# Order of the first weight loads, FFN1 by output column, and an event instruction for the last wait in a one-core decode kernel

## Chip, cores, metric

One core of one Trainium2 chip. The metric is the device time of one execution in microseconds (us), lower is better.

## The reference

A decode step: one new token for each of two sequences, with a key and value cache of 8192 positions, 32 heads of 128, and beside it a feed-forward block (FFN) on the same normed input.

```python
def reference(A_x, A_k_cache, A_v_cache, A_wq, A_wo, B_x, B_w1, B_w2):
    # x (2,1,512), caches (2,32,8192,128), wq (512,4096), wo (4096,512),
    # w1 (512,1792), w2 (1792,512), all bf16
    xn = _layernorm(A_x)
    # attention: q = xn@wq; softmax(q k^T / sqrt(128)) v; @wo
    # FFN: relu(xn@w1) @ w2
    return A_x + _A_ref(xn, A_k_cache, A_v_cache, A_wq, A_wo) + _B_ref(xn, B_w1, B_w2)
```

The caches are 268 MB of the 280.5 MB read. Each byte is used once.

## The kernel before

SyncE issues every large load, in order, on one queue. K and V come in tiles of 4 MB, one for a pair of heads, into two buffers each. TensorE transposes K, ScalarE and VectorE copy it back, TensorE makes scores and weighted values. wq borrows a V buffer, w1 and w2 share the buffer that wo takes at the end.

```python
    nc.sync.dma_start(w1_sb, B_w1.rearrange("(p kt) f -> p kt f", kt=KT)).then_inc(dW1, 16)
    nc.sync.dma_start(vs[1][:], A_wq.rearrange("(p kt) n -> p (kt n)", kt=KT)).then_inc(dV[1], 16)
    nc.scalar.dma_start(xsb[:], A_x.flatten_outer_dims()).then_inc(dX, 16)
    # SyncE, ...
        sp.dma_start(w2_sb, B_w2.rearrange("(p j) n -> p j n", j=FT)).then_inc(dW2, 16)
        load_k(0); load_k(1); load_v(0)
        for t in range(NP - 2):              # NP = 32 pairs of heads
            sp.wait_ge(pT[NG - 1], t + 1)    # K buffer transposed
            load_k(t + R)                    # R = 2
            sp.wait_ge(sW, t + 1)            # V buffer used
            load_v(t + 1)
        # ... last V in two halves, wo in five pieces, then the store of the output
    # GpSimd, at its end
        g.wait_ge(dO, 16)                    # the store has landed
        g.nop()
    # TensorE, before the loop over pairs (cut)
        pe.wait_ge(dW1, 16)
        w1_v = w1_sb.rearrange("p kt (f j) -> p kt j f", j=FT)     # step of 14 elements along f
        for g in range(FG):                                        # FFN1: w1 is the moving operand
            nj = min(4, FT - 4 * g)
            for kt in range(KT):
                i = pe.matmul(hp[:, 0:nj * P].rearrange("c (l f) -> c l f", f=P),
                    lhsT=xz[:, kt, Z - g * Bsz:Z - g * Bsz + FG * Bsz],
                    rhs=w1_v[:, kt, 4 * g:4 * g + nj, :], ...)
        pe.wait_ge(dV[1], 16)
        # ... 32 matmuls of q from wq; transposes of the hidden vector and of q; FFN2; then the loop
```

Of the kernel before, what the change touches and what calls it, by code (L numbers as in the profile page):

```python
# [7 lines left out]
ALU = mybir.AluOpType  # L8
# [11 lines left out]
def kernel(  # L20
# [12 lines left out]
    nc = tc.nc  # L33
    P = 128
    HP = P // 2
    bf16 = mybir.dt.bfloat16
    f32 = mybir.dt.float32

    Bsz, Sq, D = A_x.shape
# [3 lines left out]
    KT = D // P  # L43
    FT = Dff // P
# [7 lines left out]
    assert KT * H * Dh == SLOT  # L52
    QG = H * Dh // 512
    QH = 512 // Dh
    FG = (FT + 3) // 4
    Z = (QG - 1) * Bsz
    inv_sqrt = float(Dh) ** -0.5
    eps = 1e-5
# [3 lines left out]
    def sb(shape, dt, name):  # L62
        return ctx.enter_context(nc.sbuf_tensor(name, shape, dt))

    def ps(shape, dt, name):
        return ctx.enter_context(nc.psum_tensor(name, shape, dt))

    def sem(name):
        return tc.alloc_semaphore(name)
# [6 lines left out]
    w1_sb = w_sb[:, 0:KT * Dff].rearrange("p (kt f) -> p kt f", kt=KT)  # L76
# [3 lines left out]
    identb = sb([P, P], bf16, "identb")  # L80
# [12 lines left out]
    xz = sb([P, KT, 2 * Z + Bsz], bf16, "xz")  # L93
# [11 lines left out]
    OTn = sb([P, Bsz, H], bf16, "OTn")  # L105
    Ob = sb([H, Bsz, Dh], bf16, "Ob")
    OX = sb([P, WJ, Bsz], bf16, "OX")
    hb = sb([FG * Bsz, 512], bf16, "hb")
    hT = sb([P, 4, FG * Bsz], bf16, "hT")
    ys = sb([Bsz, D], f32, "ys")  # L110
    yT = sb([P, Bsz, KT], bf16, "yT")
    osb = sb([Bsz * KT, P], bf16, "osb")
# [1 line left out]
    tp = [ps([P, EG, P], bf16, f"tp{i}") for i in range(4)]  # L114
    Sc = [ps([P, 512], f32, f"Sc{i}") for i in range(2)]
    ot = [ps([P, 512], f32, f"ot{i}") for i in range(2)]
# [7 lines left out]
    def bc_of(i):  # L124
# [3 lines left out]
    dX, dO, dW1, dW2 = sem("dX"), sem("dO"), sem("dW1"), sem("dW2")  # L128
# [4 lines left out]
    sG, sI, sQ, sQ1 = sem("sG"), sem("sI"), sem("sQ"), sem("sQ1")  # L133
# [5 lines left out]
    sH, sF, sZ = sem("sH"), sem("sF"), sem("sZ")  # L139
# [11 lines left out]
    tpx = tp[0][:].rearrange("p g k -> p (g k)")[:, 0:KT * Bsz].rearrange(  # L151
        "p (kt b) -> p kt b", b=Bsz
    )
    hp = ot[1][0:FG * Bsz, :]
    tph = tp[2][:].rearrange("p g k -> p (g k)")[:, 0:4 * FG * Bsz].rearrange(
        "p (l c) -> p l c", l=4
    )
    y = Sc[1][0:Bsz, :]
    fin = ot[0][:, 0:KT * Bsz].rearrange("p (b c) -> p c b", c=KT)

# [4 lines left out]
    def load_v(t):  # L165
        nc.sync.dma_start(vs[t % R][:], V_all[t * P:(t + 1) * P, :]).then_inc(dV[t % R], 16)

    nc.sync.dma_start(w1_sb, B_w1.rearrange("(p kt) f -> p kt f", kt=KT)).then_inc(dW1, 16)
    nc.sync.dma_start(vs[1][:], A_wq.rearrange("(p kt) n -> p (kt n)", kt=KT)).then_inc(dV[1], 16)
    nc.scalar.dma_start(xsb[:], A_x.flatten_outer_dims()).then_inc(dX, 16)  # L170


    @(lambda f: f(nc.sync))
    def _(sp):
        sp.dma_start(w2_sb, B_w2.rearrange("(p j) n -> p j n", j=FT)).then_inc(dW2, 16)
        load_k(0)
        load_k(1)
        load_v(0)
        for t in range(NP - 2):
            sp.wait_ge(pT[NG - 1], t + 1)  # L180
            load_k(t + R)
            sp.wait_ge(sW, t + 1)
            load_v(t + 1)
        sp.wait_ge(sW, NP - 1)
        for i in range(2):
            sl = slice(i * SLOT // 2, (i + 1) * SLOT // 2)
            sp.dma_start(  # L187
                vs[(NP - 1) % R][:, sl], V_all[(NP - 1) * P:NP * P, sl]
            ).then_inc(dH[i], 16)
        for c in range(NC):  # L190
            sl = slice(cuts[c], cuts[c + 1])
            sp.dma_start(wo_sb[:, sl, :], wo_v[:, sl, :]).then_inc(dW[c], 16)  # L192
        sp.wait_ge(sE, 1)
        sp.dma_start(
            out.rearrange("b s (c p) -> (b s c) p", p=P), osb[:]
        ).then_inc(dO, 16)


    @(lambda f: f(nc.gpsimd))
    def _(g):  # L200
        g.memset(identb[:], 0.0).then_inc(sG, 1)
        g.memset(sel[:], 0.0).then_inc(sG, 1)
        g.memset(onesh[:], 0.0).then_inc(sG, 1)
        g.wait_ge(sG, 1)
        g.affine_select(
            out=identb[:], in_=identb[:], compare_op=ALU.not_equal, fill=1.0,
            base=0, pattern=[[-1, P]], channel_multiplier=1,
        ).then_inc(sI, 1)
        g.wait_ge(sG, 2)
        g.affine_select(  # L210
            out=sel[:], in_=sel[:], compare_op=ALU.not_equal, fill=1.0,
            base=0, pattern=[[-1, DQ], [1, P]], channel_multiplier=-DQ,
        ).then_inc(sI, 1)
        g.wait_ge(sI, 2)
        g.memset(prm[0][:], 0.0).then_inc(sG, 1)
        g.wait_ge(sG, 4)
        for u in range(2):
            g.memset(onesh[u * HP:(u + 1) * HP, u, :], 1.0).then_inc(sI, 1)
            g.wait_ge(sI, 3 + u)
        g.memset(ident2[:], 0.0).then_inc(sG, 1)  # L220
        g.wait_ge(sG, 5)
        g.affine_select(
            out=ident2[:], in_=ident2[:], compare_op=ALU.not_equal, fill=1.0,
            base=0, pattern=[[-1, Bsz]], channel_multiplier=1,
        ).then_inc(sI, 1)
        g.wait_ge(sV, 100)
        for t in range(NP):
            if t >= R:
                g.wait_ge(sS, t - R + 1)
            g.tensor_copy(q2[t % R][:], qb[:, 2 * t:2 * t + 2]).then_inc(sQ1, 1)  # L230
        g.wait_ge(dO, 16)
        g.nop()


    @(lambda f: f(nc.tensor))
    def _(pe):
        pe.wait_ge(sI, 1)
        pe.wait_ge(sV, 5)
        for kt in range(KT):
            i = pe.transpose(tpx[:, kt, :], xn[:, kt, :], identb[0:Bsz, 0:Bsz])  # L240
        i.then_inc(sQ, 1)
        pe.wait_ge(sV, 6)
        pe.wait_ge(dW1, 16)

        w1_v = w1_sb.rearrange("p kt (f j) -> p kt j f", j=FT)
        for g in range(FG):
            nj = min(4, FT - 4 * g)
            for kt in range(KT):
                i = pe.matmul(  # L249
                    hp[:, 0:nj * P].rearrange("c (l f) -> c l f", f=P),  # L250
                    lhsT=xz[:, kt, Z - g * Bsz:Z - g * Bsz + FG * Bsz],
                    rhs=w1_v[:, kt, 4 * g:4 * g + nj, :],
                    start=(g == 0 and kt == 0),
                    stop=(g == FG - 1 and kt == KT - 1),
                )
        i.then_inc(sF, 1)
        pe.wait_ge(dV[1], 16)
        for g in range(QG):
            for kt in range(KT):
                i = pe.matmul(  # L260
                    qp,
                    lhsT=xz[:, kt, Z - g * Bsz:Z - g * Bsz + QG * Bsz],
                    rhs=vs[1][:, (kt * QG + g) * 512:(kt * QG + g + 1) * 512],
                    start=(g == 0 and kt == 0),
                    stop=(g == QG - 1 and kt == KT - 1),
                )
        i.then_inc(sQ, 1)
        pe.wait_ge(sF, 2)
        for l in range(4):
            i = pe.transpose(  # L270
                tph[:, l, :], hb[:, l * P:(l + 1) * P], identb[0:FG * Bsz, 0:FG * Bsz]
            )
        i.then_inc(sF, 1)
        pe.wait_ge(sV, 7)
        for l in range(QH):
            i = pe.transpose(
                tpq[:, l, :], qs[:, l * Dh:(l + 1) * Dh], identb[0:QG * Bsz, 0:QG * Bsz]
            )
        i.then_inc(sQ, 1)
        pe.wait_ge(sF, 4)  # L280
        pe.wait_ge(dW2, 16)
        for j in range(FT):
            i = pe.matmul(  # L283
                y,
                lhsT=hT[:, j % 4, (j // 4) * Bsz:(j // 4 + 1) * Bsz],
                rhs=w2_sb[:, j, :],
                start=(j == 0),
                stop=(j == FT - 1),
            )
# [77 lines left out]
        pe.wait_ge(sP, NP + 1)  # L367
        pe.wait_ge(sO, NP + 1)
        pe.wait_ge(sI, 5)
        pe.wait_ge(sF, 6)  # L370
        dbp = Sc[0][:, 0:N].rearrange("p (t u) -> p t u", u=2)
        for u in range(2):
            t = pe.matmul(dbp[:, :, u], lhsT=onesh[:, u, :], rhs=RS[:], start=True, stop=True)
# [1 line left out]
        for k in range(KT):  # L375
            pe.matmul(
                fin[:, k, :],
                lhsT=ys[:, k * P:(k + 1) * P],
                rhs=ident2[:],
                start=(k == 0),  # L380
                stop=False,
# [13 lines left out]
        for dq in range(DQ):  # L395
            t = pe.matmul(
                ox,
                lhsT=sel[:, dq, :],
                rhs=Ob[:, :, dq * WJ:(dq + 1) * WJ],
                start=(dq == 0),  # L400
                stop=(dq == DQ - 1),
# [4 lines left out]
        for c in range(NC):  # L406
            pe.wait_ge(dW[c], 16)
            for j in range(cuts[c], cuts[c + 1]):
                for k in range(KT):
                    t = pe.matmul(  # L410
                        fin[:, k, :],
                        lhsT=wo_sb[:, j, k * P:(k + 1) * P],
                        rhs=OX[:, j, :],
                        start=False,
                        stop=(j == WJ - 1 and k == KT - 1),
# [13 lines left out]
    def _(v):  # L429
# [13 lines left out]
            out=xn[:],  # L443
            in0=xsb[:].rearrange("b (p kt) -> b kt p", kt=KT),
            scalar1=mv[:, 0:1],
            scalar2=rinv[:, 0:1],
            op0=ALU.subtract,
# [2 lines left out]
        v.wait_ge(sQ, 1)  # L450
        v.wait_ge(sZ, 1)
        v.tensor_copy(xz[:, :, Z:Z + Bsz], tpx).then_inc(sV, 1)
        v.wait_ge(sF, 1)
        v.tensor_scalar(  # L454
            out=hb[:], in0=hp, scalar1=0.0, scalar2=None, op0=ALU.max,
        ).then_inc(sF, 1)
        v.wait_ge(sQ, 2)

        v.tensor_scalar(  # L459
            out=qs[:], in0=qp, scalar1=inv_sqrt, scalar2=None, op0=ALU.mult  # L460
        ).then_inc(sV, 1)
        v.wait_ge(sF, 3)
        v.tensor_copy(hT[:], tph).then_inc(sF, 1)
        v.wait_ge(sQ, 3)

        v.tensor_copy(
            qb[:].rearrange("p (b g l) -> p l g b", b=Bsz, l=QH),
            tpq.rearrange("p l (g b) -> p l g b", b=Bsz),
        ).then_inc(sV, 93)
        v.wait_ge(sF, 5)  # L470
        v.tensor_tensor(out=ys[:], in0=y, in1=xsb[:], op=ALU.add).then_inc(sF, 1)

        def pair(i, n):
# [19 lines left out]
        with v.Fori(0, NP // R):  # L493
# [10 lines left out]
            out=on[:, 0:N - 2], in0=OTf[:, 2:N], in1=RD[:, 0:N - 2], op=ALU.mult  # L504
# [3 lines left out]
            out=on[:, N - 2:N], in0=ot[1][:, 0:2], in1=RD[:, N - 2:N], op=ALU.mult  # L508
# [81 lines left out]
```

## Time and profile before

| | before |
|---|---|
| median time, 3 runs | 661.67 us (661.57 to 661.88) |
| span of the profiled run | 659.7 us |
| last piece of wo landed | 655.86 us |
| from there to the end of the span | 3.86 us |

Times within a trace count from the span's start. In the page's slices one digit or number stands for a fortieth of the span. A line of the timeline gives start, length, engine, source line, operation and count; in brackets is the idle time before it and what ended it. The lines themselves stand in the prediction.

### The profile page before, as it was taken

What the parts mean: (1) busy time and instruction counts of PE and PEld (TensorE: products, weight loads), DVE (VectorE), ACT (ScalarE), POOL (GpSimd) and SP (SyncE); (2) the same over time, 40 slices, a digit from 0 to 9 for tenths busy, and PEclk for the clock granted to TensorE, in tenths of its full rate; (3) what the DMA queues carried; (4) which work ended last, traced back from release to release, by engine and by line L of the source; (5) the groups of instructions that cost most, each with busy time, mean ns of one, the idle gap of its engine ahead of it and who ended that gap; (6) DMA issues with size and microseconds to landing.
All of it is one profiled execution on the core that took longest, in us unless ns stands there. A gap on an engine that the chain in (4) does not pass through costs nothing.

```text
span 659.7 us, 26788 instructions
## 1 busy us (share of the span) xinstructions
PE 568.2 (86%) x12701; PEld 535.8 (81%) x12701; DVE 253.6 (38%) x437; ACT 255.8 (39%) x403; POOL 8.8 (1%) x46
## 2 busy tenths in 40 slices
PE   4998899979799788789878879978788898878897
PEld 0388898978798788789878879978788888878896
DVE  1154354424344333334433434443334443434341
ACT  1044445434434434244353433534243434433340
POOL 1000000000000000000000000000000000000000
PEclk9998999979999889898988998989899988989996
DMA  8999999999999999999999999999999999999996
GB/s 360 431 437 432 424 435 425 441 429 429 435 427 439 425 435 431 431 433 425 441 425 433 437 425 439 425 435 431 431 433 425 441 427 431 437 425 439 425 424 259
DMA packets 10542, 280.66 MB, mean 425 GB/s; under 512 B 1186, under 2 KB 1188, under 8 KB 1700
## 3 DMA queue, kind: packets, MB, share of 16 engines
q1 hardware_dynamic: 10528, 280.50, 99.0%
q8 instruction: 9, 0.15, 0.1%
q14 instruction: 1, 0.01, 0.0%
q10 hardware_dynamic: 4, 0.00, 0.0%
HBM read 280.50 MB, written 0.00 MB: 425 GB/s over the span
## 4 chain that ended last, share of the span: by engine, by line
DMA 59%; PE 37%; ACT 2%; issue 1%; SPq 0%; DVE 0%; ACTq 0%
DMA ks<-in_A_k_cache_dram 53%; PE tp L298 20%; PE Sc L305 10%; DMA w_sb<-in_A_wo_dram 4%; PE ot L318 3%; PE ot L249 2%; ACT kT L425 2%; PE ot L260 1%; DMA w_sb<-in_B_w_dram 1%; PE Sc L283 0%; ACT L425 0%; SPq L192 0%; SPq L187 0%; PE Sc L353 0%; DVE qs L459 0%
## 5 line engine op out<-in xcount | busy, mean ns | idle before, releaser
L298 PE MATMUL tp<-identb,ks 128*128 128x128 bf16 x4096 | 324.5, 229 | 70.1 <-DMA ks<-in_A_k_cache_dram 67.5
L425 DVE COPY kT<-tp 128x1024 bf16<-128x1024 bf16 x320 | 219.5, 691 | 322.4 <-PE tp L298 322.0
L298 PEld LDWEIGHTS tp<-identb,ks 128*128 128x128 bf16 x4096 | 255.7, 103 | 73.9 <-DMA ks<-in_A_k_cache_dram 70.7
L425 ACT COPY kT<-tp 128x1024 bf16<-128x1024 bf16 x192 | 194.3, 1012 | 236.2 <-PE tp L298 236.1
L305 PE MATMUL Sc<-q,kT 128*128 128x64 bf16 x4096 | 217.3, 196 | 6.5 <-ACT kT L425 5.6
L305 PEld LDWEIGHTS Sc<-q,kT 128*128 128x128 bf16 x4096 | 179.1, 100 | 10.0 <-ACT kT L425 9.1
L318 PE MATMUL ot<-prm,vs 128*128 128x64 bf16 x4224 | 157.4, 193 | 0.4 <-issue 0.4
L318 PEld LDWEIGHTS ot<-prm,vs 128*128 128x128 bf16 x4224 | 140.4, 98 | 3.2 <-issue 0.5
L540 ACT COPY nm<-Sc 128x2 f32<-128x2 f32 x32 | 5.1, 160 | 118.9 <-PE Sc L356 118.9
L544 ACT ACTIVATE prm<-Sc,nm 64x128 bf16<-64x128 f32 x64 | 25.7, 401 | 4.3
L481 DVE TENSOR_REDUCE mcol<-Sc 64x1 bf16<-64x128 f32 x64 | 18.6, 291 | 18.5 <-PE Sc L305 18.0
L425 ACT ACT_TABLE_LOAD x16 | 20.5, 1283 | 2.2
L486 DVE TENSOR_REDUCE mx<-Sc 1x2 bf16<-1x128 bf16 x32 | 8.9, 279 | 17.5 <-PE Sc L353 17.5
L249 PE MATMUL ot<-w_sb,xz 128*8 128x512 bf16 (+1 forms) x16 | 12.9, 975 | 3.0 <-DMA w_sb<-in_B_w_dram 3.0
L532 ACT COPY OTf<-ot 128x2 f32 x32 | 5.1, 160 | 22.4 <-PE ot L318 22.4
L230 POOL COPY q<-qb 128x2 bf16<-128x2 bf16 x32 | 5.8, 184 | 591.0 <-PE Sc L305 563.7
L249 PEld LDWEIGHTS ot<-w_sb,xz 128*8 128x8 bf16 x16 | 1.6, 104 | 13.4 <-issue 13.4
L544 ACT ACTIVATION_READ_ACCUMULATOR prm<-Sc,nm x64 | 11.8, 185 | 0.0
L260 PE MATMUL ot<-vs,xz 128*16 128x512 bf16 x32 | 8.2, 422 | 0.0
L260 PEld LDWEIGHTS ot<-vs,xz 128*16 128x16 bf16 x32 | 3.1, 98 | 5.4 <-issue 2.4
L353 PE MATMUL Sc<-identb,mcol 128*1 128x128 bf16 x32 | 7.0, 217 | 0.0
L454 DVE TENSOR_SCALAR hb<-ot 8x512 bf16<-8x512 f32 x1 | 0.7, 678 | 15.8 <-PE ot L249 15.8
(59 smaller groups left out, 39.5 us busy)
## 6 DMA issues: line engine op xcount, KB each, us to landing
ks<-in_A_k_cache_dram SPq DMA_DIRECT2D x32, 4096.0 KB, 26.7
vs<-in_A_v_cache_dram SPq DMA_DIRECT2D x31, 4096.0 KB, 31.3
vs<-in_A_wq_dram SPq DMA_DIRECT2D x1, 4096.0 KB, 17.0
vs<-in_A_v_cache_dram SPq DMA_DIRECT2D x2, 2048.0 KB, 19.0
w_sb<-in_B_w_dram SPq DMA_DIRECT2D x2, 1792.0 KB, 14.3
w_sb<-in_A_wo_dram SPq DMA_DIRECT2D x1, 1792.0 KB, 25.1
w_sb<-in_A_wo_dram SPq DMA_DIRECT2D x1, 896.0 KB, 26.8
w_sb<-in_A_wo_dram SPq DMA_DIRECT2D x1, 768.0 KB, 28.2
```

Source lines behind the costliest of these rows:

```text
L230: g.tensor_copy(q2[t % R][:], qb[:, 2 * t:2 * t + 2]).then_inc(sQ1, 1)
L249: i = pe.matmul(hp[:, 0:nj * P].rearrange("c (l f) -> c l f", f=P), lhsT=xz[:, kt, Z - g * Bsz:Z - g * Bsz + FG * Bsz], rhs=w1_v[:, kt, 4 ...
L260: i = pe.matmul(qp, lhsT=xz[:, kt, Z - g * Bsz:Z - g * Bsz + QG * Bsz], rhs=vs[1][:, (kt * QG + g) * 512:(kt * QG + g + 1) * 512], start=( ...
L298: t = pe.transpose(tp[e % 4][:, i, :], ks[r][:, kk * Dh:(kk + 1) * Dh], identb[:])
L305: t = pe.matmul(Sc[r][:, 2 * kk:2 * kk + 2 * REP], lhsT=kT[e % 4][:, i, :], rhs=rep(q2[r][:]), start=True, stop=True,)
L318: t = pe.matmul(ot[r][:, 0:2 * REP], lhsT=vs[r][:, kk * Dh:(kk + 1) * Dh], rhs=rep(prm[r][:, kk, :]), start=(kk == 0), stop=(kk == KB - 1),)
L353: pe.transpose(tr_of(r), mcol[r][:], identb[:]).then_inc(sT, 1)
L425: fn(kT[e % 4][:], tp[e % 4][:]).then_inc(kR[e], 1)
L481: m = v.tensor_reduce(out=mcol[i][half, :], in_=S_of(i)[half, :, u], axis=AX.X, op=ALU.max)
L486: v.tensor_reduce(out=mx[i][:], in_=tr_of(i).rearrange("o (u m) -> o u m", u=2), axis=AX.X, op=ALU.max, negate=True,).then_inc(sX, 1)
L532: a.copy(OTf[:, bass.ds(c, 2)], ot[r][:, 0:2]).then_inc(sO, 1)
L544: x = a.activation(out=prm[i][half, :, u], in_=S_of(i)[half, :, u], func=ACTF.Exp, bias=nm[i][half, u:u + 1], scale=1.0, accum_out=RS[half ...
```

## The change

The intent: q, which the attention needs, comes first; the FFN1 weights become the stationary operand, so that the hidden vector comes out already transposed (by column) and needs no transposes of its own; and the wait for the store is no longer carried by a branch.

```diff
-    nc.sync.dma_start(w1_sb, B_w1.rearrange("(p kt) f -> p kt f", kt=KT)).then_inc(dW1, 16)
     nc.sync.dma_start(vs[1][:], A_wq.rearrange("(p kt) n -> p (kt n)", kt=KT)).then_inc(dV[1], 16)
...
     def _(sp):
+        sp.dma_start(w1_sb, B_w1.rearrange("(p kt) f -> p kt f", kt=KT)).then_inc(dW1, 16)
         sp.dma_start(w2_sb, B_w2.rearrange("(p j) n -> p j n", j=FT)).then_inc(dW2, 16)
...
-        g.wait_ge(dO, 16)
-        g.nop()
+        g.wait_ge(dO, 16).then_inc(sG, 1)
...  (the FFN1 loop moves behind the q projection and becomes)
+        for j in range(FT):
+            for kt in range(KT):
+                i = pe.matmul(
+                    hp[:, j, :],
+                    lhsT=w1_v[:, kt, j, :],
+                    rhs=xz[:, kt, Z:Z + Bsz],
+                    start=(kt == 0),
+                    stop=(kt == KT - 1),
+                )
...  (its four transposes go; VectorE writes relu(hp) straight to hT, after q's eviction)
```

## The prediction

> **What bounds the kernel now.** I read the page first: its span, the busy shares, the slices and the queues.

> ```profile
> span 659.7 us, 26788 instructions
> ...
> PE 568.2 (86%) x12701; PEld 535.8 (81%) x12701; DVE 253.6 (38%) x437; ACT 255.8 (39%) x403; POOL 8.8 (1%) x46
> ...
> DMA  8999999999999999999999999999999999999996
> GB/s 360 431 437 432 424 435 425 441 429 429 435 427 439 425 435 431 431 433 425 441 425 433 437 425 439 425 435 431 431 433 425 441 427 431 437 425 439 425 424 259
> ...
> q1 hardware_dynamic: 10528, 280.50, 99.0%
> ```

> The reader is to see that every slice but the first and the last moves 424 to 441 GB/s and that one queue alone keeps the 16 engines busy for 99.0% of the span. TensorE is busy too (86%), so the next question is which of the two waits for the other. The view of waits answers it, first for the engines, then for the queue that issues the loads.

> ```profile
> PE tp L298 <- DMA ks<-in_A_k_cache_dram: 67.5, 27, 3.4
> ...
> SPq L163 <- PE tp L298: 435.8, 30, 40.7
> SPq L166 <- PE ot L318: 144.5, 30, 5.6
> ```

> TensorE waits 27 times for a K tile. The issuing queue waits for TensorE as well (a K buffer is reused once it has been transposed), but that is the issue, not the transfer: issued loads lie in the queue. What counts is whether the queue ever runs dry. The tightest places are early, and the timeline of the first 90 us shows them:

> ```profile
> 8.84 12.92 PE L249 MATMUL ot<-w_sb,xz 128*8 128x512 bf16 x16 [3.03 <-DMA w_sb<-in_B_w_dram]
> ...
> 21.58 8.23 PE L260 MATMUL ot<-vs,xz 128*16 128x512 bf16 x32
> ...
> 30.77 3.18 PE L283 MATMUL Sc<-w_sb,hT 128*2 128x512 bf16 x14
> ...
> 33.88 1.51 PE L298 MATMUL tp<-identb,ks 128*128 128x128 bf16 x24
> ...
> 44.82 0.33 SPq L163 DMA_DIRECT2D ks<-in_A_k_cache_dram  x1
> ...
> 53.91 0.73 PE L298 MATMUL tp<-identb,ks 128*128 128x128 bf16 x10 [2.61 <-issue]
> ...
> 65.25 0.33 SPq L163 DMA_DIRECT2D ks<-in_A_k_cache_dram  x1
> ```

> Six loads are issued at the start: w1, wq, w2, K0, K1, V0, together 2 x 1.835 + 4 x 4.194 = 20.45 MB. Data begins to flow at about 2.4 us (the windows show 8 GB/s before 2 us and 244 from 2 to 4). At 432 GB/s they last until 2.4 + 47.3 = 49.7 us. The next load, K2, is issued at 44.82, so 4.9 us of work was still in the queue. With K2 and V1 the queue has 28.84 MB and lasts until 69.2; K3 comes at 65.25, 3.9 us ahead. That is the smallest margin that I find; K4 comes at 83.17 and K5 at 99.02, with 37.2 and 45.6 MB issued, so some 5 and 9 us ahead. TensorE catches up until 99 us and waits for K in nearly every step from there. So the transfers set the time from 2.4 us until the last piece of wo lands. The chain of waits, read near the end, gives the rest:

> ```profile
> 627.04 28.82 DMA w_sb<-in_A_wo_dram
> 655.86 0.05 issue
> 655.91 0.39 PE ot L410 x8
> 656.29 0.02 issue
> 656.32 0.18 DVE yT L517
> 656.49 0.04 issue
> 656.54 0.28 PE tp L419
> ```

> The last load lands at 655.86, then a short serial tail runs to 659.72. The span is 1.95 us below the timed 661.67.

> [...] the slices average about 431. [...] the kernel has about 653.5 us between first and last byte, with instruction fetches and the uneven end of the 16 engines in it. [...] The trace before has no strided weight load; its packed ones with a moving width of 2 (L410) went at 84 in 2.36 us, 28 ns each. [...] The old FFN1 reads w1 as the moving operand with a step of 14 elements, 28 bytes[...]: 0.91 us for 512 columns, 1.78 ns a column, against 0.43 us for packed columns of the q projection just after it.

> **The change part by part.**
> First, the order of loads. The same bytes in the same number of loads; no byte leaves the queue, and the first issue stays at 0.96 us. Worth 0 on the transfer path. For TensorE it moves the first wait: w1 (1.835 MB) landed at 0.96 + 7.74 = 8.70; wq, first now, is 2.36 MB more, at 431 GB/s 5.5 us, so 14.2 us. w1 then lands where wq did, 1.43 + 17.0 = 18.4 us, and w2 stays.
> Second, TensorE's front part. From 14.2 us the 32 matmuls of q take about 8.7 us (8.23 in before with some six at 0.43 us and the rest at 0.215[...]), which ends at 22.9, after w1. Then FFN1: 56 loads of 128 weights with a step of 28 bytes, each with a matmul of 2 columns, in place of 16 wide matmuls (12.92 us), and no transposes of the hidden vector (0.25 us, and its 0.68 us eviction of 8x512 turns into one of 128x28, some 0.16 us as the small copies here). Two cases. [...] If not, 128 x 1.78 = 228 ns, 12.8 us. [...] After FFN1 come the q transposes, the eviction and FFN2: 0.25 + 0.4 + 3.2 = some 3.9 us, as the 4.1 us from 29.8 to 33.9 in before. K0's transposes begin at 22.9 + 3.2 + 3.9 = 30.0 us in the first case, 3.9 us earlier than 33.88; at 39.6 in the second, 5.7 later.
> On the path to the end, being 3.9 us earlier is worth nothing: K2 would be issued at about 41 us behind 8.8 us of queued work instead of 4.9. What TensorE gains it hands back as a longer wait for K, at the latest where it now catches up at 99 us.
> Third, the last wait. In the sequencers' records the 2 KB store's landing is complete at 658.28; GpSimd's compare-and-branch, which carries the wait, runs 658.305 to 658.338, and its next instruction, the NOP that releases the final barrier, stands at 658.467. That is 0.16 us from the branch's start. SyncE, whose last branches carry no wait, goes from the end of its store's issue (657.456) to its next instruction (657.501) in 0.045 us. With the wait on an event instruction (0.017 us in these records) and free branches behind it I reckon 0.06 us, so 0.1 us gained at the serial end, nothing beside it.
> Sum: 0 + 0 - 0.1. Prediction: 661.57, rounded to 661.6 us.

> **The rivals.**
> A: TensorE's front part is on the path. The chain of waits gives L249 2% and L260 1% of the span; whoever takes this as time to be had expects 4 to 10 us less, 652 to 658. Against it stand the flat GB/s row and the queue's backlog at 44.82; the chain only says what TensorE did while the transfers ran beside it.
> B: The strided weights go at the slow rate (or slower), and TensorE starts K0 5.7 us late. Then K2 is issued at 50.5 against 49.7, K3 at 71 against 69.2 (if the 2.61 us stall stays), and the queue runs dry for 1 to 2 us and some start-up: 663 to 665. For it: the w1 reads did cost 1.78 ns a column. Against it: [...] that q's start could hide part. I give it one in seven.
> C: The instruction fetches move. TensorE's program is some 72 instructions longer in front of the loop (40 more load-matmul pairs less 4 transposes), so the 2.61 us stall in the first pass and the 16 KB fetches among the data fall elsewhere. The early stall is hidden; a fetch on the last engine to finish could move the last landing by 0.6 us (16 KB at a sixteenth of 431 GB/s) either way: 661.0 to 662.2.
> D: The event instruction costs as much as the branch: 661.7.

> **Range and chances.** The three runs of before span 0.31 us. Around 661.6 I put C's and D's few tenths on both sides and a part of B above: 661.0 to 662.4. Over 2% faster means below 648.7[...]: excluded but for a misreading, 0.005. Over 2% slower means above 674.9, 13 us of dry queue, more than B makes: 0.01.

> **What would show it right or wrong.** The slices' GB/s stay at 424 to 441 and the last wo piece lands within 0.4 us of 655.86. The q matmuls start near 14.2 us. FFN1's 56 matmuls take near 3 us (first case) or near 13 us (second). K0's transposes start near 30 us; K2 is issued near 41, and TensorE's total wait for K grows by some 3 us. The gap from the store's landing to GpSimd's NOP shrinks from 0.19 to about 0.1 us. I am wrong if a slice early on falls below 420, if the last landing moves by more than 1 us, or if the tail after 655.86 changes by more than 0.3 us.

The 3.2 us for FFN1 in the first case stands as my estimate, which nothing in the trace before showed; with it the sum for K0 comes to 22.9 + 3.2 + 3.9 = 30.0 us. (The second case, "if not", takes the 1.78 ns that the trace has for a column at that step for each of 128 weights.) And the reason why 2% faster was excluded; an estimate from the trace does as well, since 280.5 MB at its 431 GB/s take 650.8 us, more than 648.7.

## The result

| | before | after |
|---|---|---|
| median of 6 runs | 661.62 us (661.37 to 661.88) | 660.84 us (660.68 to 661.06) |
| span of the profiled run | 659.72 | 658.64 |
| last piece of wo landed | 655.86 | 654.85 |
| from there to the end | 3.86 | 3.79 |

The ratio is 0.9989 (95% interval 0.9976 to 1.0002). A ratio is the mean time of one kernel's runs over that of the other's of the same rounds, so not quite the ratio of the medians quoted. 660.84 lies below my range. A second set of five runs of the same kernel (below) gave 660.84 again, ratio 0.9985 (0.9971 to 0.9998). Of the 1.08 us between the two spans, 1.01 is the earlier last landing and 0.07 the shorter tail.

The page after, the same parts as in the prediction:

```profile
span 658.6 us, 26859 instructions
...
DMA  8999999999999999999999999999999999999996
GB/s 365 430 444 418 439 430 429 432 428 442 422 442 424 436 428 432 432 428 444 420 442 428 432 430 430 434 430 442 424 436 428 432 432 428 440 424 442 426 424 281
...
q1 hardware_dynamic: 10528, 280.50, 99.2%
```

The stream of loads is as full as before. (A slice at 418 was to prove me wrong by my own text; these numbers swing by 20 and more from slice to slice, and counted by whole packets the 16 engines had work from 3.5 to 652 us in both traces.) The timeline of the front part after:

```profile
13.23 9.54 PE L240 MATMUL ot<-vs,xz 128*16 128x512 bf16 x32 [8.60 <-DMA vs<-in_A_wq_dram]
...
22.70 3.52 PE L253 MATMUL ot<-xz,w_sb 128*128 128x2 bf16 x56
...
26.50 5.84 PE L270 MATMUL Sc<-w_sb,hT 128*2 128x512 bf16 x14
...
32.77 1.51 PE L285 MATMUL tp<-identb,ks 128*128 128x128 bf16 x24 [0.43 <-DMA ks<-in_A_k_cache_dram]
...
43.72 0.33 SPq L158 DMA_DIRECT2D ks<-in_A_k_cache_dram  x1
```

FFN1 shrank from 12.92 to 3.52 us, 63 ns for each pair of weight load and matmul. But K0 begins only 1.1 us earlier: TensorE now waits for K0 itself, whose last part landed at 32.73. That none of this reaches the end, as forecast, is tested below. The chain of waits near the end says where the time came from:

```profile
625.73 29.12 DMA w_sb<-in_A_wo_dram
654.85 0.05 issue
654.90 0.39 PE ot L397 x8
```

The transfers end 1.01 us earlier, with the same bytes in the same number of loads (280.50 MB on the load queue in both) at the same rate (425 and 426 GB/s on average). The windows of the last four microseconds of transfer show it as well. Columns: window and its length, busy time (and count) of PE, PEld, DVE, ACT and POOL, granted clock, DMA share, GB/s. First before, then after:

```profile
652.00:653.00 1.00, 1.00 (x44) 1.00 (x41) 0.00 (x0) 0.00 (x0) 0.00 (x0) 0.50 0.88 336
653.00:654.00 1.00, 0.82 (x31) 0.73 (x28) 0.00 (x0) 0.00 (x0) 0.00 (x0) 0.50 0.50 195
654.00:655.00 1.00, 0.68 (x24) 0.68 (x24) 0.00 (x0) 0.00 (x0) 0.00 (x0) 0.50 0.26 92
655.00:656.00 1.00, 0.70 (x20) 0.53 (x18) 0.00 (x0) 0.00 (x0) 0.00 (x0) 0.50 0.05 20
```

```profile
652.00:653.00 1.00, 0.49 (x18) 0.40 (x14) 0.00 (x0) 0.00 (x0) 0.00 (x0) 1.00 0.83 326
653.00:654.00 1.00, 0.75 (x25) 0.67 (x25) 0.00 (x0) 0.00 (x0) 0.00 (x0) 0.57 0.51 201
654.00:655.00 1.00, 0.72 (x22) 0.56 (x18) 0.00 (x0) 0.00 (x0) 0.00 (x0) 0.50 0.21 70
655.00:656.00 1.00, 0.54 (x9) 0.27 (x8) 0.33 (x2) 0.00 (x0) 0.00 (x0) 0.50 0.00 0
```

In both the engines leave one by one from 652 us on. Before, a few drag on past 655; after, none does. It is not the stream that got faster but its slowest engine.

That can be read engine by engine: in the trace each large load has 16 landing records, as many as the profile counts DMA engines, and I read them as one for each. (Where a single landing is still out, in pool_fetch below, the DMA share is 0.06, one engine of 16.) Here they are (us, sorted; computed from the trace's landing events) for the first load and for the last piece of wo:

```
before, first load (w1):  7.23 7.29 7.30 7.33 7.38 7.40 7.49 7.58 7.65 7.70 7.81 7.88 8.24 8.62 8.64 8.70
after,  first load (wq): 12.70 12.79 12.86 12.89 12.90 12.91 12.93 12.94 12.95 12.96 12.97 12.98 12.99 13.00 13.07 13.09
before, last of wo: 652.98 652.99 653.08 653.09 653.36 653.37 653.42 654.31 654.45 654.50 654.62 654.77 655.05 655.44 655.84 655.86
after,  last of wo: 653.04 653.06 653.18 653.19 653.20 653.23 653.40 653.44 654.67 654.70 654.71 654.74 654.78 654.83 654.84 654.85
```

The first engine to finish wo does so at 652.98 and 653.04, no gain at all; the last at 655.86 and 654.85. The spread of the first load's landings is 1.47 us before and 0.39 after, a difference of 1.08; that of the last is 2.88 and 1.81, a difference of 1.07. In between the spread of before is 1.45 or 1.46 in the loads that land at 18 (wq), 23 (w2) and 32 us (K0). So an engine that starts late stays late: the 1.47 us at 8.70 us is still 1.45 or 1.46 at 32. (The landing records do not name the engine. That it is the same one is read from the distances between the 16 landings, which stay the same from load to load.)

The second feature of these rows is the step of about 1.3 us that splits the 16 landings of after into two groups. The trace has packets of 16 KB on an instruction queue. (I take them for TensorE fetching its program, from where they lie: in before one runs from 51.4 to 52.5 us, within TensorE's 2.61 us of "issue" from 51.30 on.) There are six before 69 us, a seventh at 107, an eighth at 650 (a ninth, at 654, comes when the engines are already leaving). V1's tile, landing at 70 us, has 6 late landings; those at 186 and 614 us have 7; the last of wo has 8. One fetch, one engine put back. Start and fetch add up where they meet on one engine: 1.47 and 1.3 come close to the 2.88 of before, 0.39 and 1.3 to the 1.81 of after.

### The profile page after: what moved, and what is told of

It is laid out like the page before. It is cut to its first block, busy times and chain, and to the rows that moved or that the text cites. A ratio compares the mean times of both kernels' runs of the same rounds, so it can differ in the third digit from the quotient of the medians.

```text
span 658.6 us, 26859 instructions
## 1 busy us (share of the span) xinstructions
PE 559.9 (85%) x12737; PEld 535.1 (81%) x12737; DVE 253.2 (38%) x436; ACT 255.8 (39%) x403; POOL 9.0 (1%) x46
## 2 busy tenths in 40 slices
DMA  8999999999999999999999999999999999999996
## 3 DMA queue, kind: packets, MB, share of 16 engines
q1 hardware_dynamic: 10528, 280.50, 99.2%
HBM read 280.50 MB, written 0.00 MB: 426 GB/s over the span
## 4 chain that ended last, share of the span: by engine, by line
DMA 58%; PE 37%; ACT 2%; issue 1%; SPq 1%; ACTq 0%; DVE 0%
DMA ks<-in_A_k_cache_dram 54%; PE tp L285 21%; PE Sc L292 11%; PE ot L305 4%; DMA w_sb<-in_A_wo_dram 4%; ACT kT L412 2%; ACT L412 1%; SPq L187 0%; PE Sc L340 0%; SPq L182 0%; PE Sc L343 0%; SPq L170 0%; SPq L169 0%; SPq L163 0%; PE ot L397 0%
## 5 line engine op out<-in xcount | busy, mean ns | idle before, releaser
L285 PE MATMUL tp<-identb,ks 128*128 128x128 bf16 x4096 | 323.5, 229 | 68.4 <-DMA ks<-in_A_k_cache_dram 68.4
L305 PEld LDWEIGHTS ot<-prm,vs 128*128 128x128 bf16 x4224 | 139.0, 97 | 7.0 <-issue 4.4
L517 ACT COPY OTf<-ot 128x2 f32 x32 | 5.1, 160 | 26.9 <-PE ot L305 26.9
L270 PE MATMUL Sc<-w_sb,hT 128*2 128x512 bf16 x14 | 5.8, 604 | 0.1
L343 PE MATMUL Sc<-mx,onesb 1*128 1x2 bf16 x32 | 5.5, 172 | 0.0
```

The costliest lines, as they stand in the source:

```text
L270: i = pe.matmul(y, lhsT=hT[:, j, :], rhs=w2_sb[:, j, :], start=(j == 0), stop=(j == FT - 1),)
L285: t = pe.transpose(tp[e % 4][:, i, :], ks[r][:, kk * Dh:(kk + 1) * Dh], identb[:])
L305: t = pe.matmul(ot[r][:, 0:2 * REP], lhsT=vs[r][:, kk * Dh:(kk + 1) * Dh], rhs=rep(prm[r][:, kk, :]), start=(kk == 0), stop=(kk == KB - 1),)
L343: pe.matmul(bc_of(r), lhsT=onesb[:], rhs=mx[r][:], start=True, stop=True).then_inc(sB, 1)
```

## The experiments

**Theories.** 1: the order of loads decides how unevenly the 16 engines start, and the slowest engine carries its delay to the end. 2: TensorE's shorter front part gives the gain. 3: only chance, the placement of instruction fetches. For each run I give the spread of the 16 landings of the first load and the last landing of wo, both worked out from the landing records as above.

### Only the order (order_only)

Base: the kernel before.

```diff
-    nc.sync.dma_start(w1_sb, ...)        # first
     nc.sync.dma_start(vs[1][:], A_wq...)
+    nc.sync.dma_start(w1_sb, ...)        # second
```

> The kernel before with one edit: wq is the first load and w1 the second. Theory 1 (the order sets how unevenly the 16 DMA engines start; the stagger of 1.47 us between the first and last engine to finish the first load of before, 0.39 after, is never absorbed because no queue runs dry): spread of the first load's 16 landings about 0.4 us, of the last wo piece about 1.8, last landing near 654.9 instead of 655.86, and 0.7 to 1.0 us faster than before. Theory 2 (TensorE's earlier start of K0, or its shorter front part, gives the gain): the old wide FFN1 now has to follow w1, K0 starts no earlier, time as before, 661.5 to 661.7. Theory 3 (only chance of the placement of instruction fetches): no rule, anywhere from 660.8 to 661.8, initial spread unrelated.

Measured: 666.58 us (before: 661.74; ratio 1.0077, 1.0064 to 1.0091), slower by some 4.8 us. The spread of the first load was 0.30 us, as theory 1 said, but the time was missed (last landing 660.51), since I had forgotten that the old program runs FFN1 ahead of q. FFN1 now waits for w1 until 17.46, takes its 12.92 us, and q, FFN2 and K0 come behind it; K2 is issued at 53.57, after the 49.7 us at which the queue of six loads is used up. The windows show the queue run dry:

```profile
48.00:50.00 2.00, 2.00 (x51) 2.00 (x48) 1.30 (x3) 1.01 (x1) 0.00 (x0) 1.00 0.65 279
50.00:52.00 2.00, 2.00 (x51) 2.00 (x49) 1.30 (x3) 1.01 (x1) 0.00 (x0) 1.00 0.08 25
52.00:54.00 2.00, 2.00 (x56) 2.00 (x54) 1.30 (x3) 1.01 (x1) 0.00 (x0) 1.00 0.00 0
54.00:56.00 2.00, 2.00 (x64) 1.88 (x61) 0.92 (x4) 0.00 (x0) 0.19 (x1) 1.00 0.98 262
```

So the prediction's rival B is a real cliff: it was only not reached by the change as a whole. And the gap gives theory 1 a free test: of the six fetches up to 80 us the two at 45 and 50 fell at or in the gap, where engines had time to catch up. The landings after it show four late engines, not six.

### All but the order (after_w1_first)

Base: the changed kernel.

```diff
+    nc.sync.dma_start(w1_sb, ...)        # first again
     nc.sync.dma_start(vs[1][:], A_wq...)
-        sp.dma_start(w1_sb, ...)
```

> The changed kernel with w1 put back as the first load, so narrow FFN1 and the event instruction alone are left of the change. Theory 1: first load's landings spread by about 1.5 us again, last wo piece lands 655.5 to 655.9 with a spread of 2.5 to 3, time 661.4 to 661.6 (the event's 0.07 us is all that is left). Theory 2: K0 starts as early as in the changed kernel or earlier, time about 660.8. Theory 3: no rule.

Measured: 662.08 us (661.52 to 664.12; before 661.74; ratio 1.0013, 0.9999 to 1.0027). First spread 1.46 us, last landing 655.86: the gain is gone, with narrow FFN1 and the event still there. Narrow FFN1 alone is therefore not the gain. Theory 2's other half, an early K0, is not tested here, though I had expected it to be: with w1 first q waits for wq until 18.5 us, and K0 starts at 35.8, later than in the kernel before. The useless loads below test it. The time is above the 661.4 to 661.6 that theory 1 gave; the runs scatter upward more than those of the kernel before. The margin of the queue is thinner with the late K0, but the traced run (661.78) had no dry spell, and what the 664.12 run did is not shown.

### The event alone (event_only)

Base: the kernel before.

```diff
-        g.wait_ge(dO, 16)
-        g.nop()
+        g.wait_ge(dO, 16).then_inc(sG, 1)
```

> The kernel before with the event instruction as its only edit. All theories: from the store's landing to the NOP that releases the final barrier 0.12 us in place of 0.19, and 0.05 to 0.1 us off the time; last wo landing as before, near 655.86, with 661.5 to 661.6. If it gains 0.5 us or more, the store's wait is worth more than the trace shows.

Measured: 661.51 us (before 661.74; ratio 0.9997, 0.9984 to 1.0011), too small for the interval. The records of GpSimd's sequencer show the step itself, in the kernel before and after the whole change:

```
before  658.282 store landed   658.305 0.033 COMPARE_BRANCH (waits)   658.467 NOP (releases the barrier)
after   657.27  store landed   657.296 0.017 EVENT_SEMAPHORE (waits)  657.392 NOP
```

From the start of the waiting instruction to the NOP it is 0.162 us with the branch and 0.096 with the event: 0.07 us, where I had reckoned 0.1. The trace of event_only itself has 0.095, and 3.79 us from the last landing to the end, as the changed kernel. Its first spread was 1.28 us, last landing 655.68: w1 first again, and again far above wq first.

### Another tensor first (after_w2_first)

Base: the changed kernel; w2 moves to the front, then wq, w1.

```diff
+    nc.sync.dma_start(w2_sb, ...)        # first
     nc.sync.dma_start(vs[1][:], A_wq...)
         sp.dma_start(w1_sb, ...)
-        sp.dma_start(w2_sb, ...)
```

> The changed kernel with w2, not wq, as the first load (then wq, then w1). It asks what makes the stagger within theory 1. If short rows do it (14336 bytes a row, as w1, against 32768 of wq): first load's spread 1.2 to 1.6 us and time 661.3 to 661.6. If it is something of w1 alone: spread about 0.4 and 660.8 to 661.0.

Measured: 662.24 us (661.06 to 663.06; ratio 1.0006, 0.9992 to 1.0019); first spread 1.32 us, as short rows would have it, last landing 656.10; the time is above the 661.3 to 661.6 expected. It is not w1 as such. w1 and w2 have in common the size (1.835 MB), rows of 14336 bytes, and rows that lie one behind the other.

### The changed kernel again (after_again)

No edit.

> The changed kernel unedited, for a second trace and for times on the chip of this group. If the stagger comes from the kernel and not from chance: first load's 16 landings spread by 0.3 to 0.4 us again (0.39 and, with only the order changed, 0.30 so far), last wo piece spread 1.8, last landing 654.7 to 655.0, 660.6 to 661.1. If by chance: a spread above 1 us.

Measured: 660.84 us (before, in this group, 661.90; ratio 0.9985, 0.9971 to 0.9998). First spread 0.63 us, twice what I expected, last landing 655.06 (above my 655.0). So the start has a scatter of its own, but stays well below that of w1 first.

### A slice of wq first (wq_slice_first, wq_slice_again)

Base: the changed kernel.

```diff
-    nc.sync.dma_start(vs[1][:], wq_v).then_inc(dV[1], 16)
+    nc.sync.dma_start(vs[1][:, 0:7168], wq_v[:, 0:7168]).then_inc(dQ, 16)
+    nc.sync.dma_start(vs[1][:, 7168:SLOT], wq_v[:, 7168:SLOT]).then_inc(dV[1], 16)
     # TensorE waits for both
```

> The changed kernel with wq loaded in two pieces: first the first 7168 columns (128 rows of 14336 bytes, as w1's, out of wq's rows of 32768), then the other 9216 columns. If the length of the rows of the first load makes the stagger: first load's spread 1.2 to 1.5 us, last landing 655.6 to 656.0, time 661.3 to 661.7 or more. If it is where w1 and w2 lie in memory (rows one after the other 14336 bytes apart): spread about 0.4, last landing near 654.9, 660.7 to 661.0.

Measured: 660.95 us (660.78 to 661.86; ratio 0.9986), first spread 0.87 us. The last landing, 656.01, misleads: this trace is of the slowest run, in which K4 was issued at 88.51 us, when the queue's 37.2 MB were just used up (2.4 + 37.2 / 0.432 = 88.5). By the packets the stream lost 0.8 us against before between 80 and 100 us. So it was repeated:

> The sliced wq once more, since its first trace fell in its slowest run (661.86; the other four 660.78 to 661.22): a first-load spread of 0.5 to 0.9 us, and if nothing runs dry at 89 us a last landing of 655.0 to 655.4 and 660.8 to 661.2 us. A spread of 1.2 or more would put it with w1 and w2.

Measured: 661.03 us (660.99 to 661.23; before 661.64; ratio 0.9990, 0.9976 to 1.0003), first spread 0.42 us, last landing 655.08. Rows as short as w1's don't make the stagger by themselves; the expectation of 661.3 to 661.7 for them is missed.

### A useless load first (dummy_flat, dummy_flat_again, dummy_slice)

Base: the changed kernel. To hold everything fixed but the place of the rows in memory, a load that nobody reads goes first: 128 rows of 14336 bytes of wq, either adjacent or at wq's distance of 32768. The output stays right.

```diff
+    nc.sync.dma_start(dum[:], wq_f[0:P * 7168].rearrange("(p c) -> p c", c=7168)).then_inc(dQ, 16)   # flat
+    nc.sync.dma_start(dum[:], wq_v[:, 0:7168]).then_inc(dQ, 16)                                      # or: slice
     nc.sync.dma_start(vs[1][:], wq_v).then_inc(dV[1], 16)
     # TensorE waits for dQ as well
```

> The changed kernel with a load of no use in front of all others: the first 1.835 MB of wq, read as 128 rows of 14336 bytes that lie one behind the other, as w1's rows do, into a buffer that nobody reads. 4.2 us of transfer more, so about 665 us; only the spread of the first load's 16 landings is asked for. So far: 1.28 to 1.47 us with w1 or w2 first, 0.30 to 0.85 with wq's 32768-byte rows, 0.87 with a slice of wq. If short adjacent rows make the stagger: 1.2 to 1.5. If it is the tensors w1 and w2: below 0.9.

> The adjacent short rows once more for a second trace: same spread as the first, within 0.3 us; about 665 us.

> The same with the useless first load taken as the first 14336 bytes of each of wq's 32768-byte rows. Short rows alone: 1.2 to 1.5 us of spread. Short rows only when they lie one behind the other: 0.3 to 0.9, as the 0.87 of the sliced wq. Time about 665 us.

Measured:

| | first spread | first and last landing of wo's last piece | time, two runs |
|---|---|---|---|
| rows adjacent | 1.36 | 657.10 and 660.11 | 665.97, 665.76 |
| the same again | 1.39 | 657.18 and 660.05 | 665.91, 665.81 |
| rows 32768 apart | 0.35 | 657.36 and 659.19 | 665.19, 665.13 |

The chains of waits end so, with the adjacent rows and then with the rows apart:

```profile
631.29 28.82 DMA w_sb<-in_A_wo_dram
660.11 0.05 issue
```

```profile
630.44 28.75 DMA w_sb<-in_A_wo_dram
659.19 0.05 issue
```

Same number of bytes, same number and length of rows, same tensor, otherwise the same program: only which rows are read, and so their distance, differs, and with it the start's spread by 1.0 us, the last landing by 0.9 and the time by 0.7 us. The pair also settles the rest of theory 2: K0 starts at 36.93 and 37.74 us with the adjacent rows and at 37.16 with the rows apart, and K2 and K4 are issued latest with the rows apart, so the kernel that ends earlier is not the one whose TensorE is ahead. (The rows apart have one trace only.) The second expectation of dummy_slice (short rows only when one behind the other) holds, that of short rows alone falls.

### The wide FFN1 behind q (wide_q_first)

Base: the changed kernel, with the old FFN1 loop, its transposes and its eviction back, but behind the q projection.

```diff
-        for j in range(FT): ...                       # 56 narrow matmuls
+        for g in range(FG): ...                       # 16 wide matmuls, after q
+        pe.wait_ge(sF, 2); 4 transposes of hb
```

> The changed kernel with the old wide FFN1 (and its transposes) back, but behind the q projection, so wq first is kept. It asks whether the narrow FFN1 is needed. By the backlog count: q ends at 22.7, wide FFN1 takes 12.9, then 0.3 and 3.2 to 5.8: K0 starts at 39.5 to 42, K2 is issued 10.9 us after that, 50.5 to 53, after the queue's 49.7: the queue runs dry for 1 to 4 us with restart, time 661.8 to 665. If TensorE's front part had no part in it: 660.8.

Measured: 665.15 us (664.68 to 666.74; before 661.90; ratio 1.0057, 1.0043 to 1.0070), just over the range given. First spread 0.56 us, last landing 659.27. K0 begins at 41.77, K2 is issued at 52.71, and the stream falls to 25 GB/s between 50 and 52 us:

```profile
50.00:52.00 2.00, 2.00 (x51) 2.00 (x48) 0.69 (x1) 1.62 (x2) 0.00 (x0) 1.00 0.08 25
52.00:54.00 2.00, 2.00 (x65) 2.00 (x62) 1.43 (x3) 0.34 (x1) 0.02 (x1) 1.00 0.66 180
```

So narrow FFN1 does not give the gain, but it is what makes wq first affordable: 4.3 us lie between this kernel and the changed one.

### More instruction fetches (pool_fetch)

Base: the changed kernel.

```diff
             g.tensor_copy(q2[t % R][:], qb[:, 2 * t:2 * t + 2]).then_inc(sQ1, 1)
+            if 6 <= t < 18:
+                for c in range(100 * (t - 6), 100 * (t - 5)):
+                    g.memset(scr[:, c:c + 1], 0.0)     # 1200 in all, each 1 element
```

> The changed kernel with 1200 one-element memsets of GpSimd on spare time, 100 after each of twelve of its q copies, so that its program has to fetch more instruction blocks in mid-stream. In the changed kernel seven 16 KB fetches of TensorE stand beside seven landings that are 1.3 us later than the rest. If each fetch delays the one DMA engine that carries it: fetch packets between 110 and 340 us, each followed by one engine falling back (0.6 to 1.3 us by size); the last landing moves by up to 1.3 us if one hits an engine already late, else stays at 654.9. If fetches do not do it: same 16 landings pattern as the changed kernel.

Measured: 665.47 us (before 661.90; ratio 1.0054, 1.0040 to 1.0068), 4.6 us over the changed kernel of the same group, far more than the 1.3 that I allowed. GpSimd had time to spare (3.35 us of memsets in a gap of some 16). Its queue of instruction packets, in the changed kernel and here:

```profile
q14 instruction: 1, 0.01, 0.0%
```

```profile
q14 instruction: 11, 0.09, 0.0%
```

```profile
655.00:656.00 1.00, 0.60 (x24) 0.51 (x20) 0.00 (x0) 0.00 (x0) 0.00 (x0) 0.50 0.06 26
656.00:657.00 1.00, 0.91 (x28) 0.82 (x28) 0.00 (x0) 0.00 (x0) 0.00 (x0) 0.50 0.06 25
657.00:658.00 1.00, 0.14 (x5) 0.14 (x6) 0.00 (x0) 0.00 (x0) 0.00 (x0) 0.50 0.13 41
658.00:659.00 1.00, 0.84 (x30) 0.76 (x29) 0.00 (x0) 0.00 (x0) 0.00 (x0) 0.50 0.06 23
```

A DMA share of 0.06 is one engine of 16, working on alone (the 0.13 has a late instruction fetch in it). This is the claim of theory 1 made by hand: 0.08 MB on one engine of a saturated stream of 280 MB costs 0.7% of the time. It also says what of theory 3 is true: fetches count, and where they land decides what they cost (ten on one engine 4.4 us here; TensorE's, one to an engine, 1.3 us each in the landings).

### All starts beside one another

| first load | first spread, us (one number a trace) |
|---|---|
| w1 or w2, rows adjacent | 1.47, 1.46, 1.28, 1.32 |
| useless load, rows adjacent | 1.36, 1.39 |
| wq, rows of 32768 | 0.39, 0.30, 0.63, 0.56, 0.85 |
| 14336 bytes of each row of wq | 0.87, 0.42, 0.35 |

No trace of the first two rows comes below 1.28, none of the others over 0.87. The spread of wo's last piece goes with it: 2.80 to 3.02 us in the six traces of the first two rows, 1.81 to 2.24 in the others except pool_fetch (6.39). No version came out that beats both kernels clearly: taking the fetches' 1.3 us away would need a TensorE program that isn't fetched during the stream, and none of the runs has one.

## Why the prediction was right or wrong

- **The bound: right.** The loads set the time; every experiment that moved the time did it by the last landing: from there to the measured time of the traced run it is 5.7 to 6.0 us in all 14 traces.
- **"The order of loads ... Worth 0 on the transfer path": wrong, and this is the step that failed.** I counted bytes and loads of the queue as one stream. The landings show 16, and the kernel waits for the slowest: TensorE's last piece of wo starts 0.05 us after the last landing in the traces of both kernels. The start was 1.08 us less uneven and it ended 1.01 us earlier. I had even written "the uneven end of the 16 engines", and took it only for a place where a fetch might fall (rival C), not as something the first load sets. The mean of the 16 landings of wo's last piece moved by only 0.2 us (654.20 to 653.99): an average over the engines hides this. The last landing moved by 1.01 us, just past the 1 us that the prediction itself names as a sign of being wrong.
- **TensorE's front part: FFN1 right, other terms mis-sized, one wait overlooked, no effect.** wq landed at 13.1, not 14.2, since I had scaled from the last of w1's 16 landings, which had the stagger in it. FFN1 took 3.52 us against 3.2 (the first case), 63 ns a pair of weight load and matmul at a mean granted clock of 0.84, so the second case's 228 ns a load did not come. (Packed weights, with a matmul of 2 columns too, went at 28 ns a pair at 0.61 in the trace before.) q took 9.54 against 8.7. FFN2 took 5.84 against 3.2; the granted clock was down to 0.53 there:

```profile
22.70:26.20 3.50, 3.50 (x58) 3.49 (x58) 0.68 (x1) 0.00 (x0) 0.00 (x0) 0.84 1.04 449
26.50:32.30 5.80, 5.79 (x14) 1.60 (x14) 0.44 (x1) 0.00 (x0) 0.30 (x2) 0.53 1.04 444
```

  Why the clock was down is not shown by a run. But it is not what held K0 up. K0 began at 32.8 instead of 30.0 because its own last part landed at 32.73, after FFN2 had ended at 32.34; in after_again, wq_slice_first and wq_slice_again, too, K0 starts within 0.05 us of its landing (32.95, 32.86 and 32.98). The prediction left this wait out: by the count behind its 49.7 us, w1, wq, w2 and K0 are 12.06 MB, which at 432 GB/s last until 30.3 us, and the trace before has K0 landing from 30.96 to 32.41. K2 followed at 43.7 instead of 41.
- **"TensorE's total wait for K grows by some 3 us": wrong,** it went from 67.5 (in the prediction) to 68.4:

```profile
PE tp L285 <- DMA ks<-in_A_k_cache_dram: 68.4, 27, 3.4
```

  K0 was only 1.1 us ahead, and TensorE's idle times put down to "issue" in the first passes (2.65 us at 68.0, 1.5 at 48.6, 1.2 at 56.2; in before 2.6 at 51.3 and two short ones) took that lead back by 71 us. That they are waits for instructions is my reading of the fetches beside them.
- **The margins of the queue: right for the first step, run-dependent after.** K2's 49.7 us was confirmed by two kernels that crossed it. But K3 is not always the tightest place: K4, due by 88.5 us, was issued at 83.2 and 83.6 in the two kernels' traces, 86.7 in the second trace of the changed one, and 88.5 in a trace that did run dry. TensorE's stalls move from run to run.
- **The last wait: right, 0.07 us for 0.1.**
- **Rival A: refuted.** after_w1_first has narrow FFN1 and no gain, and with the useless loads the kernel that issues K2 and K4 later ends earlier.
- **Rival B: right as a mechanism** (order_only, wide_q_first), and not what happened.
- **Rival C: real, but its size was wrong.** A 16 KB fetch was to cost its engine 0.6 us; it cost 1.3 in the landings. The early ones stay in the last landing too. Both kernels have nine of them, so they are not what moved.
- **The range** was too narrow below, because its low end held only a few tenths for rival C and nothing for the order of loads.

Left open: why adjacent rows of 14336 bytes make the engines start unevenly. The runs vary the distance of the rows (14336 or 32768 bytes) and find the effect; whether adjacency, alignment or something else of their place does it, none tells. Also not shown is how an engine is chosen for a fetch.

## What to carry to other kernels

In a kernel that keeps the load queue full from start to end, look at the 16 landings of the first and the last load, not only at GB/s: what one engine lost here (1.47 us against 0.39 in the first load, 1.3 us by an instruction fetch of 16 KB, some 6.5 us by ten of 8 KB) was still there in the last landings. In order_only, where the queue ran dry between 50 and 54 us, late engines did catch up (four late ones after it for six fetches). Start with a load whose landings come close together, and don't pad any engine's program, idle engines' too, with instructions that must be fetched during the stream: GpSimd's 1200 memsets on spare time cost 4.6 us. When a reordering moves a consumer, count the bytes queued ahead against the issue time of the next load; two kernels here fell off that edge by 3 to 4 us, and were 4.3 and 5.7 us slower than the changed kernel.
